# Turning the keys of a decode attention on VectorE instead of TensorE

## The chip, the cores and the metric

The kernel runs on one core of a Trainium2 chip. The metric is the device time of one execution in microseconds, the median of several executions. The profile is of one execution, taken by the hardware profiler; its span runs from the first to the last instruction of the program. The engines are named as the profile names them: PE (TensorE), DVE (VectorE), ACT (ScalarE), POOL (GpSimd), SP (SyncE, whose queue issues nearly all DMAs here).

## The reference

One decode step of grouped-query attention plus a token mixer, both on the same normalised input, in float32:

```python
B, D, HQ, HKV, SK, DH, F = 8, 512, 32, 8, 8192, 128, 1792   # one query position
xn = layernorm(x)                                  # (8, 1, 512)
q  = xn @ wq                                       # 32 query heads of 128
s  = einsum(q, k_cache) * DH**-0.5                 # 4 query heads share a K/V head
o  = softmax(s) @ v_cache                          # over 8192 positions
y  = gelu(layernorm(xn) * w1 + b1) @ w2 + b2       # the mixer: w1 is (1, 1792), w2 (1792, 1)
out = x + o @ wo + y
```

The two caches are (8, 8, 8192, 128) each: 64 pairs of batch element and K/V head, 4 MiB of keys and 4 MiB of values to a pair. Every key and value is used once, for four query rows.

## The kernel before, in words

The 64 pairs are the items, numbered i = h * 8 + b (h the K/V head, b the batch element). A cache tile of an item has 128 partitions and holds 64 rows of 128 numbers in each: partition p has positions 64p to 64p + 63. It comes by one DMA of 4 MiB into one of the five buffers of the pool `ring`. `load_next` (L72) takes the next load of a list that is sorted beforehand (L58 to L61) and is called whenever a buffer has been read for the last time: after an item's last key transpose (L213) and after its last value matmul (L292). SP issues each load as soon as its buffer is free.

The scores need the head dimension on partitions. So keys are transposed first, in chunks of 16 tiles (four chunks an item): `t_half` (L201) does eight 128x128 transposes on PE into a PSUM tile (L209) and copies the 128x1024 result to SBUF (L210), one half of a chunk on ACT, the other on DVE. `qk` (L217) then multiplies: four matmuls a chunk, each with 32 stationary columns and 512 moving ones, into the four 32-row bands of one PSUM tile (L227). The stationary operand is a window on the mostly zero tile Z, which puts the four heads' scores of chunk c into their own rows.

The softmax of an item is a chain of small steps: the row maximum on DVE (L235), a matmul that lays it along the free dimension (L240), a minimum over the rows of the same head on DVE (L243), the exponential with its row sums on ACT (L249), four PE transposes (L256) and a copy on ACT (L257) that make the weights of the value matmuls, and a matmul with a reciprocal (L264, L266) for the sum. `pv` (L272) does four matmuls a chunk (L283). At an item's end ACT scales the result (L296), four small matmuls pick the used blocks (L308), and a DVE copy puts them in the head's tile (L310). After 8 items `o_project` (L312) multiplies with that head's rows of wo (L316) and DVE adds to the sum (L318). The mixer runs beside this, 14 steps a batch element: a GELU on ACT (L335), two operations on POOL (L336, L337).

The order of the work is written out by hand, and each engine executes its instructions in that order. A global step s is one chunk; in each step the order on PE is the two half chunks of transposes of chunk s + 1, `qk` of chunk s, `pv` of chunk s - 9, and what the hooks (L352 to L370) put behind each of these. So three items are in work at a time: one whose keys are turned and multiplied, one in its softmax, one whose values are multiplied. The very last value tile comes in five pieces and its last chunk has matmuls of its own (L288), ahead of the last `o_place`, `o_project` and the output's DMA (L396).

## Time and profile before

| what | value |
|---|---|
| median of 3 runs | 1310.31 us (1308.93 to 1311.67) |
| span of the profiled execution | 1308.7 us |
| that execution against the median of the runs | 1.6 us under it |
| PE, DVE, ACT, POOL busy | 1160.2, 411.6, 586.8, 227.1 us |
| HBM read | 553.69 MB, 423 GB/s over the span |
| mean granted PE clock | 0.962 of full speed |

A matmul in float32 shows as two instructions in the profile, so 16 matmuls are 32 rows; transposes are single. PE's busy time is from modelled ends of pipelined instructions, and the granted clock tells what the throttle let through, 1.00 being full speed. Matmuls that write different 32-row bands overlap: a group of eight instructions (four matmuls) is one unit in the timeline.

### The profile page before, as it was taken

Reading aid. Unit: us, or ns where it says so; the run is one execution under the profiler, and the core shown is the slowest. Engines: PE = TensorE matmul, PEld = TensorE weight load, DVE = VectorE, ACT = ScalarE, POOL = GpSimd, SP = SyncE. Lnnn points to the kernel's source line nnn. Section 1 sums busy time; section 2 is a strip of 40 time slices with the busy share of each in tenths; the row PEclk is TensorE's granted clock in tenths of the full one; section 3 lists DMA queues with packets and bytes.
Section 4 is the critical chain, followed back from the end, with each engine's and each line's share of the span. In section 5 each row is a group of like instructions: output and inputs, shape, how many; then the busy total and the mean of one; then the engine's idle time right before and its main releaser. Section 6 shows DMA issues by size and latency. Waiting matters only on the chain.

```text
span 1308.7 us, 22310 instructions
## 1 busy us (share of the span) xinstructions
PE 1160.2 (89%) x9852; PEld 718.3 (55%) x9852; DVE 411.6 (31%) x640; ACT 586.8 (45%) x734; POOL 227.1 (17%) x242
## 2 busy tenths in 40 slices
PE   3999899988899889988899898899889897999978
PEld 2655555545556555555555555555555555555544
DVE  2433233333233322333323233233233332323321
ACT  0555335553265433554345552455425544345522
POOL 1132102320032200322002220032101221013210
PEclk9999899999999989999899999899989999989999
DMA  9999999999999999999999999999999999999994
GB/s 401 431 431 426 438 432 432 432 431 432 432 432 432 428 430 432 433 431 429 432 430 432 433 431 432 432 432 431 431 433 432 431 431 433 431 434 433 428 428 178
DMA packets 24229, 555.13 MB, mean 424 GB/s; under 512 B 2461, under 2 KB 2493, under 8 KB 6981
## 3 DMA queue, kind: packets, MB, share of 16 engines
q1 hardware_dynamic: 23988, 553.67, 98.5%
q8 instruction: 77, 1.26, 0.4%
q14 instruction: 20, 0.16, 0.0%
q0 software_dynamic: 128, 0.02, 0.0%
q10 hardware_dynamic: 16, 0.02, 0.0%
HBM read 553.69 MB, written 0.02 MB: 423 GB/s over the span
## 4 chain that ended last, share of the span: by engine, by line
DMA 63%; PE 34%; ACT 2%; issue 1%; DVE 0%; SPq 0%; ACTq 0%; DVEq 0%
DMA raw<-in_A_k_cache_dram 62%; PE pt L209 15%; PE acc L227 7%; PE acc L283 6%; PE misc L308 3%; DMA raw<-in_A_wq_dram 2%; ACT L249 1%; PE pt L179 1%; PE misc L325 1%; ACT kt L210 1%; PE misc L316 1%; PE misc L256 0%; ACT t2k L249 0%; PE misc L240 0%; PE misc L264 0%
## 5 line engine op out<-in xcount | busy, mean ns | idle before, releaser
L209 PE MATMUL pt<-ident,raw 128*128 128x128 f32 x4096 | 523.1, 284 | 94.7 <-DMA raw<-in_A_k_cache_dram 93.8
L209 PEld LDWEIGHTS pt<-ident,raw 128*128 128x128 f32 x4096 | 481.8, 148 | 102.8 <-issue 90.8
L210 DVE COPY kt<-pt 128x1024 f32<-128x1024 f32 x256 | 313.5, 1225 | 660.7 <-PE pt L209 531.1
L210 ACT COPY kt<-pt 128x1024 f32<-128x1024 f32 x256 | 258.8, 1011 | 486.0 <-PE pt L209 323.6
L227 PE MATMUL acc<-kt,z 128*32 128x512 f32 x2048 | 283.0, 626 | 0.0
L283 PE MATMUL acc<-raw,pt 128*32 128x512 f32 x2040 | 266.2, 594 | 5.1 <-DMA raw<-in_A_v_cache_dram 5.1
L336 POOL TENSOR_SCALAR g<-g,w2t 128x512 f32<-128x512 f32 x112 | 77.5, 692 | 824.9 <-ACT g L335 824.9
L283 PEld LDWEIGHTS acc<-raw,pt 128*32 128x32 f32 x2040 | 64.9, 111 | 154.4 <-issue 134.1
L337 POOL TENSOR_TENSOR macc<-macc,g 128x512 f32<-128x512 f32 x112 | 142.4, 1271 | 9.3
L335 ACT ACTIVATE g<-hb,b1t,w1t 128x512 f32<-128x512 f32 x112 | 91.1, 813 | 9.8 <-POOL macc L337 9.2
L296 ACT ACTIVATE t2k<-acc,rl 128x512 f32<-128x512 f32 (+1 forms) x65 | 44.1, 679 | 109.0 <-PE acc L283 105.1
L308 PEld LDWEIGHTS misc<-ohu,t2k 128*128 128x128 f32 x512 | 61.9, 191 | 54.2 <-DVE kt L210 35.2
L256 PEld LDWEIGHTS misc<-ident,t2k 128*128 128x128 f32 x256 | 26.8, 140 | 79.4 <-ACT t2k L249 78.5
L308 PE MATMUL misc<-ohu,t2k 128*128 128x4 f32 x512 | 67.5, 255 | 0.6 <-ACT t2k L296 0.6
L227 PEld LDWEIGHTS acc<-kt,z 128*32 128x32 f32 x2048 | 41.1, 110 | 45.9 <-issue 45.9
L256 PE MATMUL misc<-ident,t2k 128*128 128x128 f32 x256 | 42.0, 286 | 22.7 <-ACT t2k L249 22.7
L249 ACT ACT_TABLE_LOAD x48 | 61.6, 1283 | 0.8
L335 ACT ACT_TABLE_LOAD x48 | 61.6, 1283 | 0.8
L257 ACT COPY pt<-misc 128x256 f32<-128x256 f32 x64 | 23.7, 370 | 57.5 <-PE misc L256 57.5
L264 PEld LDWEIGHTS misc<-lr,ohl 128*128 128x128 f32 x128 | 19.0, 188 | 53.7 <-issue 39.4
L240 PEld LDWEIGHTS misc<-ident,mr 128*128 128x128 f32 x128 | 19.0, 187 | 53.7 <-DVE kt L210 38.6
L235 DVE TENSOR_REDUCE mr<-acc 128x1 f32<-128x512 f32 x64 | 43.7, 683 | 7.0 <-PE acc L227 6.8
(68 smaller groups left out, 249.0 us busy)
## 6 DMA issues: line engine op xcount, KB each, us to landing
raw<-in_A_k_cache_dram SPq DMA_DIRECT2D x63, 4096.0 KB, 30.0
raw<-in_A_v_cache_dram SPq DMA_DIRECT2D x63, 4096.0 KB, 33.5
raw<-in_A_wq_dram SPq DMA_DIRECT2D x2, 4096.0 KB, 12.6
wo<-in_A_wo_dram SPq DMA_DIRECT2D x8, 1024.0 KB, 32.4
raw<-in_A_k_cache_dram SPq DMA_DIRECT2D x4, 1024.0 KB, 26.8
raw<-in_A_v_cache_dram SPq DMA_DIRECT2D x1, 2048.0 KB, 30.4
raw<-in_A_v_cache_dram SPq DMA_DIRECT2D x1, 1024.0 KB, 32.5
raw<-in_A_v_cache_dram SPq DMA_DIRECT2D x1, 512.0 KB, 33.2
```

The costliest lines, as they stand in the source:

```text
L209: nc.tensor.transpose(pt[:, t * P:(t + 1) * P], KR[n // NCH][:, n % NCH * CH_T + k * w + t, :], ident)
L210: (nc.vector.tensor_copy if k else nc.scalar.copy)(KT[n][:, k * w * P:(k + 1) * w * P], pt)
L227: nc.tensor.matmul(S[i][j * GW:(j + 1) * GW, :], w, kt[:, j * 512:(j + 1) * 512], start=(c == 0), stop=(c == NCH - 1))
L235: nc.vector.tensor_reduce(mr, S[i], AX.X, ALU.max)
L249: nc.scalar.activation(p, S.pop(i), AF.Exp, bias=st[i], scale=SCALE, accum_out=lr)
L256: nc.tensor.transpose(m[:, u * P:(u + 1) * P], p[:, u * P:(u + 1) * P], ident)
L283: nc.tensor.matmul(O[i][j * GW:(j + 1) * GW, :], w, v[:, j * 512:(j + 1) * 512], start=(c == 0), stop=(c == NCH - 1))
L296: nc.scalar.activation(ob[:, x], o[:, x], AF.Copy, scale=rl)
L308: nc.tensor.matmul(m[:, :REP], ob[:, u * DH:(u + 1) * DH], ohu[:, u * REP:(u + 1) * REP], start=(u == 0), stop=(u == GT - 1))
L335: nc.scalar.activation(g, hb, AF.Gelu_apprx_tanh, bias=b1t[:, j:j + 1], scale=w1t[:, j:j + 1])
L336: nc.gpsimd.tensor_scalar(g, g, w2t[:, j:j + 1], 1.0, op0=ALU.mult, op1=ALU.mult)
L337: nc.gpsimd.tensor_add(acc, acc, g)
```

## The change

The keys are no longer transposed by PE through PSUM. `turn` lets DVE transpose a quarter of an item's keys (128 partitions by 16 tiles of 128, 2048 numbers in each partition) in place in the ring buffer, in blocks of 32x32. After that the head dimension is on partitions only within blocks of 32: partition 32i + d holds component d of a quarter j of the head dimension for the positions of partition band i. So `qk` runs over the four quarters j of the head dimension, with 16 matmuls as before, each reading 16 runs of 32 numbers of the turned tile; its stationary operand W has the query's quarter j in the four bands (`QT` now holds each quarter copied to all bands, by four more matmuls in each half of `q_project`). An item's `qk` starts when its four turns are done, and frees the buffer (`load_next` is called after it).

The softmax keeps its maximum, bias and exponential. Its row sums go to a tile of the head (`LR`). The four transposes and the ACT copy become one matmul with a permutation matrix (512 columns) and one DVE block transpose out of PSUM. The value matmuls are 16 with 512 columns, as before. The result is not scaled on ACT: DVE masks it (128x512), adds halves (256, then 128 columns), one matmul picks, and the scaling by the sums is done once a head (`o_sums`, `o_scale`).

The order is no longer one of chunks with a lag: an item's scores, softmax and values follow one another, and the four turns of the next item stand between them. The last two items have an order of their own. The loads alternate keys and values, except that the last keys come ahead of the last two value tiles; wo of the last head comes behind the last values, in four pieces, and wo of the head before in two.

```diff
@@ load_next, load_wo
-        order.append((i * NCH - 1, kc, KR, i))
-        order.append((i * NCH + LAG, vc, VR, i))
+        order.append((2 * i, kc, KR, i))
+        order.append((2 * i + (1 if i < N_IT - 2 else 2.5), vc, VR, i))
...
+            if not order:
+                load_wo(HKV - 1)
...
+        if h < HKV - 1:
+            for p in (slice(0, 8), slice(8, P)) if h == HKV - 2 else (slice(0, P),):
+                nc.sync.dma_start(t[p], rows[p])
+        else:
+            for r in range(REP):
+                nc.sync.dma_start(t[:, r, :], rows[:, r, :])
@@ t_half goes (PE transposes and the copies to SBUF), turn comes
+    def turn(i, a, w=NT // 4):
+        if i < N_IT:
+            t = KR[i][:, a:a + w, :].rearrange("p t d -> p (t d)")
+            nc.vector.transpose(t, t)
+    def qk(i):
+        h, b = divmod(i, B)
+        S[i] = ps_s.tile([P, 512], F32, name="s")
+        kt = KR.pop(i).rearrange("p (u g) d -> p g u d", g=NG)
+        for j in range(NB):
+            for g in range(NG):
+                nc.tensor.matmul(S[i][g * Q:(g + 1) * Q, :], W[h % 2][:, b, j, :], kt[:, g, :, j * Q:(j + 1) * Q],
+                                 start=(j == 0), stop=(j == NB - 1))
+        load_next()
@@ sm_place: four transposes and an ACT copy go
+        m = misc()
+        nc.tensor.matmul(m, perm, st.pop(i), start=True, stop=True)
+        PT[i] = work.tile([P, 512], F32, name="pt")
+        nc.vector.transpose(PT[i], m)
@@ sm_sum and the scaling on ACT go; four picks become one
+    def o_pick(i):
+        om = t2k.tile([P, 512], F32, name="t2k")
+        nc.vector.tensor_tensor(om.rearrange("p (g d) -> p g d", g=NG), O.pop(i).rearrange("p (g d) -> p g d", g=NG),
+                                dm.unsqueeze(2).to_broadcast([P, NG, DH]), ALU.mult)
+        ob = work.tile([P, 256], F32, name="ob")
+        nc.vector.tensor_add(ob, om[:, :256], om[:, 256:])
+        nc.vector.tensor_add(ob[:, :DH], ob[:, :DH], ob[:, DH:])
+        OB[i] = ob
...
+        nc.tensor.matmul(MH[h][:, b * REP:(b + 1) * REP], OB.pop(i)[:, :DH], sel, start=True, stop=True)
...
+    def o_sums(h):
+        m = misc()
+        for r in range(REP):
+            nc.tensor.matmul(m[:, r * B:(r + 1) * B], sel[:, r:r + 1].to_broadcast([P, P]), LR[h % 2], start=True, stop=True)
+        RD[h] = work.tile([P, REP, B], F32, name="rd")
+        nc.vector.reciprocal(RD[h], m[:, :REP * B].rearrange("p (r b) -> p r b", r=REP))
+
+    def o_scale(h):
+        nc.vector.tensor_tensor(OTS[h % 2].rearrange("p r (b s) -> p r b s", s=BS)[:, :, :, 0],
+                                MH.pop(h)[:, :REP * B].rearrange("p (b r) -> p r b", r=REP), RD.pop(h), ALU.mult)
@@ the order of the work, instead of the hooks and the loop over chunks
+    for i in range(N_IT - 2):
+        h, b = divmod(i, B)
+        if i == 0:
+            for a in range(4):
+                turn(0, a * quart)
+        qk(i)
+        sm_max(i)
+        sm_bias(i)
+        sm_exp(i)
+        sm_place(i)
+        turn(i + 1, 0)
+        pv(i)
+        if b == 0:
+            mx_begin(h)
+        k = 2 if h + 1 < HKV else 3
+        for j in range(k * b, min(k * b + k, NF)):
+            mx_step(h, j)
+        turn(i + 1, quart)
+        o_pick(i)
+        turn(i + 1, 2 * quart)
+        o_place(i)
+        if b == B - 1:
+            o_sums(h)
+            mx_end(h)
+        if b == 2:
+            load_wo(h) if h < HKV - 1 else None
+        if 3 <= b < 3 + NB and h + 1 < HKV:
+            q_place(h + 1, b - 3)
+        turn(i + 1, 3 * quart)
+        if b == B - 1:
+            o_scale(h)
+            o_project(h)
+    h = HKV - 1
+    i, e = N_IT - 2, N_IT - 1
+    qk(i)
+    sm_max(i)
+    sm_bias(i)
+    sm_exp(i)
+    sm_place(i)
+    for a in range(4):
+        turn(e, a * quart)
+    pv(i)
+    qk(e)
+    o_pick(i)
+    sm_max(e)
+    sm_bias(e)
+    sm_exp(e)
+    sm_place(e)
+    o_place(i)
+    o_sums(h)
+    mx_end(h)
+    for u0, u1 in ((0, 8), (8, 12), (12, 14), (14, 16)):
+        pv(e, u0, u1)
+    o_pick(e)
+    o_place(e)
+    o_scale(h)
+    o_project(h)
```

## The prediction

> **What bounds the kernel now.** First the page's head, its slices of DMA rate, and the waits.

> ```profile
> span 1308.7 us, 22310 instructions
> PE 1160.2 (89%) x9852; PEld 718.3 (55%) x9852; DVE 411.6 (31%) x640; ACT 586.8 (45%) x734; POOL 227.1 (17%) x242
> DMA  9999999999999999999999999999999999999994
> GB/s 401 431 431 426 438 432 432 432 431 432 432 432 432 428 430 432 433 431 429 432 430 432 433 431 432 432 432 431 431 433 432 431 431 433 431 434 433 428 428 178
> ...
> q8 instruction: 77, 1.26, 0.4%
> ...
> raw<-in_A_k_cache_dram SPq DMA_DIRECT2D x63, 4096.0 KB, 30.0
> ```
> ```profile
> PE pt L209 <- DMA raw<-in_A_k_cache_dram: 93.8, 43, 5.4
> ```

> The DMA engines are full at 432 GB/s from the second slice to the last but one, and PE, busy as it is, waits 43 times for keys. An item needs 2 x 4.194 MB, which is 19.42 us at 432 GB/s; an eighth of a head's wo (1.05 MB) adds 0.30. So **19.7 us an item** is the floor of any order of the work: a loop that stays under it gains only at the ends, one that goes over it pays 64 times its excess.

> **What the change removes.** 64 PE transposes an item, their copies on two engines, and the overlap of three items. The rows of the groups:

> ```profile
> L209 PE MATMUL pt<-ident,raw 128*128 128x128 f32 x4096 | 523.1, 284 | 94.7 <-DMA raw<-in_A_k_cache_dram 93.8 <-ACT g L335 0.6 <-ACT kt L210 0.2
> ...
> L210 DVE COPY kt<-pt 128x1024 f32<-128x1024 f32 x256 | 313.5, 1225 | 660.7 <-PE pt L209 531.1 <-issue 75.6 <-ACT g L335 46.5
> L227 PE MATMUL acc<-kt,z 128*32 128x512 f32 x2048 | 283.0, 626 | 0.0
> ...
> L235 DVE TENSOR_REDUCE mr<-acc 128x1 f32<-128x512 f32 x64 | 43.7, 683 | 7.0 <-PE acc L227 6.8
> ...
> L318 DVE TENSOR_TENSOR yacc<-misc,yacc 128x128 f32<-128x128 f32 x8 | 2.3, 291 | 5.5 <-PE misc L316 5.5
> ...
> L116 DVE COPY t2k<-oh 128x128 f32<-128x128 f32 x1 | 0.2, 226 | 0.0
> ```

> PE falls by 523 us of transposes. That is worth nothing in itself, since PE is not the floor. What decides is the new order on the in-order engines. On DVE the maximum of item i stands behind the four turns of item i (done in the pass of item i - 1), and waits for `qk`; behind it wait bias, the weights' transpose, two turns, `o_pick`, two turns. On PE `qk` of the next item waits for the last turn. So nothing of two items overlaps except `pv` with two turns, and the period is one closed chain: qk, maximum, bias, minimum, exponential, permutation, transpose, the longer of pv and two turns, pick, two turns.

> **The price of a turn** (2048 columns; no such operation in the trace). DVE needs 683 ns for 512 columns (L235) and 1225 for 1024 (L210), 1.06 ns a column: 1.225 + 1024 x 1.06 ns = 2.31 us. Lower bound: SBUF to SBUF the copy L116 takes 226 ns for 128 columns where L318 takes 291; with the same fixed 155 ns (291 - 128 x 1.06) that is 0.55 ns a column, so 1.3 us. Upper bound: POOL's 1271 ns for 512 columns, quoted below, is 2.48 ns a column, 5.1 us. I take 2.3, the row of the same engine and the longest stream. [...]

> **The other links** come from the last softmax, where nothing but its own chain ran:

> ```profile
> 1287.06 1.07 PE L227 MATMUL acc<-kt,z 128*32 128x512 f32 x8
> ...
> 1287.94 1.04 PE L283 MATMUL acc<-raw,pt 128*32 128x512 f32 x8
> ...
> 1288.19 0.69 DVE L235 TENSOR_REDUCE mr<-acc 128x1 f32<-128x512 f32 x1 [0.86 <-PE acc L227]
> ...
> 1290.89 0.49 PE L240 MATMUL misc<-ident,mr 128*128 128x128 f32 x2
> ...
> 1291.42 0.29 DVE L243 CUSTOM_DVE_ANT_0 sq<-misc,hmask 128x128 f32<-128x128 f32 x1 [1.25 <-PE misc L240]
> ...
> 1291.75 0.69 ACT L249 ACTIVATE t2k<-acc,nb 128x512 f32<-128x512 f32 x1
> ...
> 1292.58 0.66 PE L256 MATMUL misc<-ident,t2k 128*128 128x128 f32 x4 [0.21 <-ACT t2k L249]
> ```
> ```profile
> 47.56 1.12 PE L325 MATMUL misc<-hn,ident 8*128 8x512 f32 x2
> ...
> 48.72 0.59 ACT L327 COPY hb<-misc 128x512 f32<-128x512 f32 x1 [1.86 <-PE misc L325]
> ```

> Groups of four matmuls follow at 0.88 us, and the reader starts 1.13 after the last one: qk or pv is 3 x 0.88 + 1.13 = 3.77. (The moving keys are now 16 runs of 32; L227 and L283 cost alike on contiguous data, the trace bounds this only from below.) Maximum 0.74 with its semaphore; bias 0.53; minimum 0.33; exponential 0.83; permutation, two passes of 512 columns as L325, 1.16; transpose of 512 out of PSUM 0.69; pick 0.69 + 0.42 + 0.29 + 0.05 = 1.45 (512, 256 and 128 columns). At full clock: 3.77 + 0.74 + 0.53 + 0.33 + 0.83 + 1.16 + 0.69 + 4.6 (two turns, over pv's 3.77) + 1.45 + 4.6 = **18.7 us**. Beside it, per head:

> ```profile
> L196 DVE COPY z<-qt x16: 174/179/1287, 34.3 to 1071.9; 128x32 f32<-128x32 f32 x16
> ```
> ```profile
> L337 POOL TENSOR_TENSOR macc<-macc,g 128x512 f32<-128x512 f32 x112 | 142.4, 1271 | 9.3
> ```
> ```profile
> 1304.08 1.08 PE L316 MATMUL misc<-wo,ot 128*32 128x128 f32 x32 [0.26 <-DVE ot L310]
> 1305.23 0.29 DVE L318 TENSOR_TENSOR yacc<-misc,yacc 128x128 f32<-128x128 f32 x1 [1.20 <-PE misc L316]
> 1305.55 0.69 SPq L396 DMA_DIRECT2D out_dram<-yacc  x1
> ```

> Eight placing copies at about 0.25 (four times L196's columns, a quarter of its partitions; its longest, 1287 ns, is as long as a POOL addition) and, at the last item, projection 1.15 plus four short DVE operations of 0.29 at most: (2.0 + 2.3) / 8 = 0.55 an item. Sum 19.25, under 19.7. So at full clock the DMA would stay the floor, by half a microsecond.

> **The clock** is what speaks against it. Nine windows at the throttle's own boundaries (PE busy first, granted clock after POOL):

> ```profile
> 189.91:193.32 3.41, 1.04 (x10) 0.73 (x7) 0.17 (x1) 0.00 (x0) 0.00 (x0) 1.00 0.94 404
> 193.32:196.74 3.42, 3.42 (x19) 2.67 (x20) 0.46 (x1) 1.01 (x1) 0.00 (x0) 0.50 1.00 431
> 196.74:200.15 3.41, 3.41 (x25) 1.17 (x17) 1.46 (x2) 0.58 (x1) 0.00 (x0) 1.00 1.00 432
> 1104.68:1108.10 3.42, 0.44 (x6) 0.30 (x2) 0.17 (x1) 0.00 (x0) 0.00 (x0) 1.00 1.02 441
> 1108.10:1111.51 3.41, 2.29 (x11) 2.32 (x12) 0.00 (x0) 0.27 (x1) 0.00 (x0) 0.50 1.07 461
> 1111.51:1114.92 3.41, 3.41 (x19) 1.55 (x21) 1.35 (x2) 0.74 (x1) 0.00 (x0) 0.50 1.04 447
> 1114.92:1118.34 3.42, 3.42 (x32) 2.62 (x24) 0.74 (x2) 0.60 (x1) 0.00 (x0) 1.00 0.99 422
> 1241.22:1244.63 3.41, 1.72 (x18) 0.50 (x10) 1.04 (x2) 1.90 (x2) 1.31 (x2) 1.00 0.91 390
> 1244.63:1248.05 3.42, 1.85 (x16) 1.73 (x16) 0.00 (x0) 0.71 (x1) 0.64 (x1) 1.00 1.04 434
> ```
> ```profile
> 1112.80 1.94 PE L227 MATMUL acc<-kt,z 128*32 128x512 f32 x8
> ...
> 1114.50 1.24 PE L283 MATMUL acc<-raw,pt 128*32 128x512 f32 x8
> ```

> A window with PE busy 1.04 of 3.41 us is followed by one at half clock; one with 1.72 is not. Back at full clock it goes after a window filled to 3.41, not after one with 2.29. At half clock a group takes 1.70 (1112.80 to 1114.50) instead of 0.88. The new loop has about 3.5 + 3.5 + 1.2 us of PE work in 19.7, 42%, and it lies badly: from the end of pv to the next qk are pick and two turns, 6.05 us with one four-column matmul. Wherever the boundaries fall, one window there has at least half of these, 3 us, idle. So every qk starts at half clock. Between qk and pv are 4.3 us with bias and permutation in them, some 1.3 busy: mostly the same. A burst starting at a random place runs slow to the end of its own window if it fills most of that (one start in five, 3.1 us), or through the next one too (4.8 us on average): 4.4 together, of which half, 2.15 us, is lost. qk and pv become 5.9, bias and permutation 0.1 and 0.4 longer.

> [...]

> **The sum.** 5.9 + 0.74 + 0.63 + 0.33 + 0.83 + 1.56 + 0.69 + 5.9 (over two turns' 4.6) + 1.45 + 4.6 = 22.6, and 0.55: **23.2 us an item**, 3.5 over the floor. Start: the first keys are there at about 34 and DVE comes to them at 38, behind the larger query projection; four turns: 47. Then 62 x 23.2 = 1438. The last two items, from the first's qk: 5.9 + 4.8 to the permuted weights, four turns 9.2 beside pv, qk 5.9, 4.8, pv 5.9, then pick, place, scale, project and add 3.5, and the output 3.2 as above (1305.55 to the span's end): 43. Span 1528; the profiled execution of before lies 1.6 under its median, so **1530 us**.

> **Costed at nothing**, with cover: the loads (SP's issue for the next key buffer now waits for qk's end, with the load for the next value buffer behind it; but with a loop slower than the DMA the ring is full; if the loop were faster, three tiles are under way, 29 us of transfer, against a wait of about 15 from keys landed to qk's end); wo's order and pieces (six more issues on SP, behind which only the output waits); the mixer, two steps an item: GELUs, POOL and table switches need some 6 us of the 18 between two exponentials; without that cover up to 1.3 an item. The trimmed tail matters only if the DMA is the floor.

> **Rivals.** (a) The clock costs under 0.5 us an item and DMA stays the floor. For it: 19.25 against 19.7, and DVE has no other work. Against: all the windows above. The end: the last values landed at 1263.8 + 33.5 = 1297.3 (rows below); wo now behind them frees 2.4, half of the instructions' 1.26 MB (q8) at 432 GB/s 1.5; then last matmuls 0.7, pick 1.45, place 0.5, scale 0.3, projection and addition 1.45, output 3.2: span 1301, **1303 us**, faster. It decides where the chain is under 19.7 us.

> ```profile
> L81 SPq DMA_DIRECT2D raw<-in_A_v_cache_dram x68: 327/328/1469, 31.6 to 1263.8; - x68
> ```
> ```profile
> raw<-in_A_v_cache_dram SPq DMA_DIRECT2D x2, 256.0 KB, 33.5
> ```

> (b) The clock falls only once an item, before qk: pv hides under two turns, the permutation is at full clock, 22.6 - 1.3 - 0.5 = 20.8, 21.4 with the rest: 47 + 62 x 21.4 + 41 = **1415 us**. (c) Turns at the lower bound 1.3: 22.6 - 2.0 + 0.55 = 21.1, **1390 us**. (d) Turns at the upper bound 5.1: both pairs 10.2, 32.5 + 0.55: about **2170 us**.

> **Chances.** Forecast 0.48 (its own range 1470 to 1585), (a) 0.27, (b) 0.12, (c) 0.08, (d) 0.03, no change to be measured 0.02. A measurement of this kernel tells 0.2%, 2.6 us, from no change. Faster 0.26, same 0.03, slower 0.71. The range takes in (a) to (c): 1298 to 1580, leaving out a fast end, a loop that locks on seven windows of 3.41 us (23.9, about 1573) with a slow start, and (d).

> **What would show it.** Granted clock about 0.7 and below 0.8 with first groups of each qk at 1.70; DMA share near 0.85 in all slices; DVE waiting for PE at the maximum and at the pick; turns at 2.3. A granted clock above 0.95, or turns well under 2 us, would make it wrong; so would a DMA share of 9 in all slices.

## The result, and the profile after

The changed kernel takes **1578.6 us** (median of 4 runs, 1576.5 to 1579.0); the kernel before, on the same chip, 1311.0 (median of 4). The ratio is **1.2045**, 95% interval 1.2028 to 1.2062: slower by 268 us, where the prediction said 219. First the page's head and its slices.

```profile
span 1576.9 us, 12454 instructions
...
PE 928.2 (59%) x5172; PEld 267.0 (17%) x5172; DVE 796.9 (51%) x835; ACT 289.0 (18%) x364; POOL 229.5 (15%) x244
...
PEclk9676677776777767776677776776768777776768
DMA  9999888998888988899889988899888998898880
GB/s 407 430 432 389 353 333 348 370 387 333 346 357 365 370 346 359 345 376 371 334 333 377 382 346 346 342 363 386 360 333 345 374 369 350 333 369 336 336 330 1
...
raw<-in_A_k_cache_dram SPq DMA_DIRECT2D x63, 4096.0 KB, 12.3
```

The loads are no longer the limit: most slices show 333 to 390 GB/s where before had 431, and a load of keys lands 12.3 us after its issue instead of 30.0: SP now issues a load only every 12 us or so (a load of values at 727.02 us, one of keys at 739.45), so little is queued ahead of it. But no engine is full either: PE 59%, DVE 51%. The row PEclk (the granted clock of TensorE in tenths) is mostly sixes and sevens: 0.736 in the mean, where the kernel before had 0.962. Time that nothing fills is waiting, and the chain says whose. One item of it, from the chain of waits of the changed kernel between 724 and 752 us (start, length, what):

```profile
727.02 0.70 DVE mr L232
...
727.77 0.50 PE misc L237 x2
...
728.40 0.29 DVE sq L240
...
728.78 1.28 ACT L246
...
730.08 0.79 ACT t2k L246 x2
...
730.91 1.34 PE misc L253 x2
...
732.27 0.73 DVE pt L255
...
733.05 6.39 PE o L266 x32
...
739.46 0.70 DVE t2k L277
...
740.99 0.39 PE mh L288 x2
741.37 4.67 issue
746.04 5.01 PE s L222 x32
...
751.07 0.70 DVE mr L232
```

From maximum to maximum it is 24.05 us, and every link of the predicted chain is there, in its order. The 4.67 us called "issue" are PE waiting for nothing that this view can name. The timeline of the same place names it:

```profile
740.85 2.30 DVE L212 STREAM_TRANSPOSE raw<-raw 128x2048 f32<-128x2048 f32 x1
...
743.17 0.45 DVE L205 COPY w<-qt 32x128 f32<-32x128 f32 x2
743.63 2.31 DVE L212 STREAM_TRANSPOSE raw<-raw 128x2048 f32<-128x2048 f32 x1
```

Two turns, with two copies of the next head's queries between them; the score product (746.04 in the chain) follows. The groups give the means, and beside them stands the one link that the prediction did not have:

```profile
L212 DVE STREAM_TRANSPOSE raw<-raw 128x2048 f32<-128x2048 f32 x256 | 577.1, 2282 | 0.3
L222 PE MATMUL s<-raw,w 128*32 128x512 f32 x2048 | 359.3, 864 | 254.0 <-issue 221.8
L266 PE MATMUL o<-raw,pt 128*32 128x512 f32 x2048 | 370.3, 890 | 51.0 <-DVE pt L255 51.0
...
L246 ACT ACT_TABLE_LOAD x55 | 70.6, 1283 | 799.7 <-DVE nb L240 799.6
L253 PE MATMUL misc<-t2k,perm 128*128 128x512 f32 x128 | 96.2, 840 | 147.5 <-ACT t2k L246 147.5
```
```profile
L249 ACT ACT_TABLE_LOAD x48 | 61.6, 1283 | 0.8
```

In the trace a load of a table (ACT_TABLE_LOAD) stands before each exponential that follows a GELU, and before each GELU that follows an exponential (54 of each in the changed kernel). The exponential's table is loaded in 55 of 64 items, the first one, ahead of which no GELU ran, among them. In the kernel before ACT stood idle for 0.8 us in all ahead of these loads; now for 799.7, of which 799.6 end with the minimum (nb). The 799.7 us cost nothing by themselves. What costs is the 1.28 us that begin when they end: in the chain above, 728.78 to 730.08. The list of waits says how many loads are caught so:

```profile
ACT L246 <- DVE nb L240: 799.6, 47, 21.2
...
ACT t2k L246 <- DVE nb L240: 243.1, 17, 22.6
```

47 loads begin only when the minimum is there. In the other 17 items it is the exponential itself that waits: nine need no load, and in eight, the second item of each head, the load runs right behind the GELU (460.31 us), 7.5 us ahead of its exponential (467.85), and costs nothing. What sets these eight apart was not tried.

### The profile page after: what moved, and what is told of

It is laid out like the page before. It is cut to its first block, busy times and chain, and to the rows that moved or that the text cites. A ratio compares the mean times of both kernels' runs of the same rounds, so it can differ in the third digit from the quotient of the medians.

```text
span 1576.9 us, 12454 instructions
## 1 busy us (share of the span) xinstructions
PE 928.2 (59%) x5172; PEld 267.0 (17%) x5172; DVE 796.9 (51%) x835; ACT 289.0 (18%) x364; POOL 229.5 (15%) x244
## 4 chain that ended last, share of the span: by engine, by line
PE 59%; issue 17%; DVE 15%; ACT 7%; DMA 1%; DVEq 0%; ACTq 0%; SPq 0%
PE o L266 24%; PE s L222 23%; PE misc L253 6%; ACT L246 4%; ACT t2k L246 3%; DVE pt L255 3%; DVE mr L232 3%; DVE t2k L277 3%; DVE raw L212 2%; PE misc L237 2%; DVE ob L280 2%; DMA raw<-in_A_wq_dram 1%; PE mh L288 1%; DVE ob L281 1%; DVE sq L240 1%
## 5 line engine op out<-in xcount | busy, mean ns | idle before, releaser
L212 DVE STREAM_TRANSPOSE raw<-raw 128x2048 f32<-128x2048 f32 x256 | 577.1, 2282 | 0.3
L222 PE MATMUL s<-raw,w 128*32 128x512 f32 x2048 | 359.3, 864 | 254.0 <-issue 221.8
L266 PE MATMUL o<-raw,pt 128*32 128x512 f32 x2048 | 370.3, 890 | 51.0 <-DVE pt L255 51.0
L328 POOL TENSOR_SCALAR g<-g,w2t 128x512 f32<-128x512 f32 x112 | 77.7, 694 | 1071.9 <-ACT g L327 1071.9
L232 DVE TENSOR_REDUCE mr<-s 128x1 f32<-128x512 f32 x64 | 44.3, 691 | 363.4 <-PE s L222 363.4
L246 ACT ACT_TABLE_LOAD x55 | 70.6, 1283 | 799.7 <-DVE nb L240 799.6
L253 PE MATMUL misc<-t2k,perm 128*128 128x512 f32 x128 | 96.2, 840 | 147.5 <-ACT t2k L246 147.5
L222 PEld LDWEIGHTS s<-raw,w 128*32 128x32 f32 x2048 | 90.0, 152 | 466.7 <-issue 433.7
L255 DVE STREAM_TRANSPOSE pt<-misc 128x512 f32<-128x512 f32 x64 | 45.9, 717 | 217.4 <-PE misc L253 217.4
L266 PEld LDWEIGHTS o<-raw,pt 128*32 128x32 f32 x2048 | 82.1, 155 | 351.8 <-issue 227.3
L327 ACT ACTIVATE g<-hb,b1t,w1t 128x512 f32<-128x512 f32 x112 | 91.1, 813 | 127.4 <-POOL macc L329 126.7
L277 DVE TENSOR_TENSOR t2k<-o,dm 128x512 f32<-128x512 f32 x64 | 44.2, 691 | 100.8 <-PE o L266 100.8
L246 ACT ACTIVATE t2k<-s,nb 128x512 f32<-128x512 f32 x64 | 44.0, 687 | 243.6 <-DVE nb L240 243.1
L327 ACT ACT_TABLE_LOAD x54 | 69.3, 1283 | 1.4
L240 DVE CUSTOM_DVE_ANT_0 sq<-misc,hmask 128x128 f32<-128x128 f32 x64 | 18.6, 291 | 44.2 <-PE misc L237 44.2
## 6 DMA issues: line engine op xcount, KB each, us to landing
raw<-in_A_v_cache_dram SPq DMA_DIRECT2D x63, 4096.0 KB, 12.8
raw<-in_A_k_cache_dram SPq DMA_DIRECT2D x63, 4096.0 KB, 12.3
raw<-in_A_wq_dram SPq DMA_DIRECT2D x2, 4096.0 KB, 17.1
```

What stands on the lines that cost most here:

```text
L212: nc.vector.transpose(t, t)
L222: nc.tensor.matmul(S[i][g * Q:(g + 1) * Q, :], W[h % 2][:, b, j, :], kt[:, g, :, j * Q:(j + 1) * Q], start=(j == 0), stop=(j == NB - 1))
L232: nc.vector.tensor_reduce(mr, S[i], AX.X, ALU.max)
L246: nc.scalar.activation(p, S.pop(i), AF.Exp, bias=st[i], scale=SCALE, accum_out=LR[h % 2][:, b:b + 1])
L253: nc.tensor.matmul(m, perm, st.pop(i), start=True, stop=True)
L255: nc.vector.transpose(PT[i], m)
```

## The experiments

Two theories had to be told apart from the start. **Theory**: one item's steps wait for each other in a closed line, TensorE's links in it run partly at half clock, and the table load is one more link. **Rivals**: the turned keys are slow to read (16 runs of 32), the turns are too much work, or the clock itself is the bound. Times below are medians, "before" is the kernel before in the same session (1310.3 to 1311.5 us), intervals are 95%.

### 1. TensorE kept busy

```diff
+    def extra(n):      # n groups of 4 matmuls, 128x32 by 512, into a tile that nobody reads
...
         sm_exp(i)
+        extra(2)
         sm_place(i)
         turn(i + 1, 0)
         pv(i)
+        extra(1)
...
         o_place(i)
...
+        extra(4)
```

> The changed kernel with TensorE kept busy while it waits: groups of four 128x32 x 512 matmuls whose result no instruction reads, two groups an item behind the exponential's issue, one behind the value product, four behind the placing of the result. Nothing of the changed kernel is left out. Theory (an open chain whose TensorE links run at a halved clock because TensorE idles for more than half of the item): the granted clock goes above 0.95 (0.736 without the groups), the score product and the value product take 3.8 and 4.6 us instead of 5.7 and 5.9, the permutation 1.2 instead of 1.55; the item falls from 24.0 to about 20.3 us and the time to 50 + 62 x 20.3 + 36 = 1345 us (1320 to 1400). Rival (the longer products come from the keys' strided columns or from the turns sharing the keys' memory, and the clock has no part in it): the products keep their 5.7 and 5.9 us, and the time stays at 1577 us or grows by the added matmuls.

Measured: **1365.9 us**, 1.0419 (1.0403 to 1.0434). More work on TensorE makes the kernel 213 us faster. The two products in the groups of this run:

```profile
L231 PE MATMUL s<-raw,w 128*32 128x512 f32 x2048 | 240.5, 610 | 57.6 <-issue 54.0
L275 PE MATMUL o<-raw,pt 128*32 128x512 f32 x2048 | 236.4, 602 | 51.0 <-DVE pt L264 51.0
```

The score product's mean falls from 864 ns to 610, the value product's from 890 to 602, although the keys lie just as they did. So the clock made them long, not the strided columns or the turns beside them. The granted clock is 0.982. The time is 21 us above the forecast, 0.3 an item. In the trace it lies at the heads' ends: from an item's maximum to the next are 18.8 to 20.5 us within a head (a little less at the very end), but 24.2 to 26.8 behind its last item. What takes the time there was not tried.

### 2. The table loaded early

```diff
         for j in range(k * b, min(k * b + k, NF)):
             mx_step(h, j)
+        nc.scalar.activation(pre[:, 1:2], pre[:, 0:1], AF.Exp)   # one column, read by nobody
```

> The changed kernel with one added ScalarE instruction an item: an exponential of a single column, whose result no instruction reads, behind the mixer's gelu steps, so that the table of the exponential is loaded while ScalarE waits for nothing. Nothing is left out. Theory (the table load that stands between the minimum and the exponential is a link of the chain, 1.36 us there against 0.33 without it): the item falls by 1.03 us to 22.96, and the time to about 1513 us (1490 to 1525). Rival (the items stay locked to the clock's windows, 56 of them in eight items, so that what one link gives up is lost in waiting or in slower matmuls): 1577 us, the period of eight items stays 191.1 us.

Measured: **1543.0 us**, 1.1769 (1.1751 to 1.1786). Neither: 36 us of the 64 came. The table load is off the chain (its line idles 1.0 us in all), and TensorE's groups took part of the gain back:

```profile
L224 PE MATMUL s<-raw,w 128*32 128x512 f32 x2048 | 386.8, 925 | 255.7 <-issue 223.5
L268 PE MATMUL o<-raw,pt 128*32 128x512 f32 x2048 | 344.3, 834 | 50.9 <-DVE pt L257 50.9
...
L255 PE MATMUL misc<-t2k,perm 128*128 128x512 f32 x128 | 114.1, 988 | 88.3 <-ACT t2k L248 88.3
...
L378 ACT ACT_TABLE_LOAD x54 | 69.3, 1283 | 1.0
```

Score product 864 to 925 ns, permutation 840 to 988, value product 890 to 834. TensorE's instructions are the same in both; the change lies in where they start within the clock's windows: for the score products of one head, between 0.02 and 0.60 of a window in the changed kernel and between 0.20 and 0.93 in this run, and the same in each of the six heads between the first and the last. The timeline shows how firmly the loop is tied to the windows: the maximum of an item and of the one eight later, in the changed kernel and in this run.

```profile
703.07 0.69 DVE L232 TENSOR_REDUCE mr<-s 128x1 f32<-128x512 f32 x1 [5.35 <-PE s L222]
```
```profile
894.22 0.69 DVE L232 TENSOR_REDUCE mr<-s 128x1 f32<-128x512 f32 x1 [5.35 <-PE s L222]
```
```profile
708.98 0.69 DVE L234 TENSOR_REDUCE mr<-s 128x1 f32<-128x512 f32 x1 [6.62 <-PE s L224]
```
```profile
896.71 0.69 DVE L234 TENSOR_REDUCE mr<-s 128x1 f32<-128x512 f32 x1 [6.62 <-PE s L224]
```

191.15 us and 187.73 us. A window of the throttle is 3.413 us in the prediction's rows (six of them are 20.48 us in those at the end of this document), and in the trace of the changed kernel 255 of the 256 stretches of one granted clock, all but the final one, are a whole number of windows long; so these are 56.0 and 55.0 windows. The loop falls into step with the windows, eight items at a time (single items run from 22.1 to 25.7 us), and the link taken out of it paid one whole window: 3.4 us for eight items, where six loads of 1.28 us, 7.7, were taken out. For the 48 items from the seventh to the 55th maximum that makes 20.5 us; the rest of the 36 came in the first and last items, where the step does not hold.

### 3. Both

```diff
+        extra(1)   # behind the exponential; 1 behind pv, 4 behind o_place
...
+        nc.scalar.activation(pre[:, 1:2], pre[:, 0:1], AF.Exp)
```

> Both additions at once: the added matmul groups (one behind the exponential's issue, one behind the value product, four behind the placing of the result; nobody reads them) and the early exponential of one column. Nothing is left out. Theory (chain and table load add up): the chain is 20.3 - 1.0 = 19.3 us an item, below the 19.7 us in which the loads can bring one item; the time falls back on the loads, 1303 to 1320 us, level with the kernel before, with the DMA share at 9 tenths in every slice. Rival (turning keys by VectorE costs time by itself, beside clock and table): 1380 us or more.

Measured: **1327.6 us**, 1.0123 (1.0106 to 1.0140). The slices of the rate in this run:

```profile
GB/s 398 437 428 423 432 432 430 430 427 431 428 432 433 426 428 429 434 431 426 429 429 434 428 429 431 428 432 427 431 431 428 430 360 396 433 431 428 430 427 118
```

The loads are the floor again, at the rate of before in nearly every slice, so the theory's sum holds. The 7.6 us over its upper end (1320) can be put down to slices 33 and 34: 360 and 396 GB/s for 33.1 us each cost (72 + 36) / 432 x 33.1 = 8.3 us. Runs 7 to 10 show where that comes from.

### 4. The same instructions with two items in work

```diff
-        order.append((2 * i + (1 if i < N_IT - 2 else 2.5), vc, VR, i))
+        order.append((2 * i + (2.5 if i != N_IT - 3 else 4.3), vc, VR, i))
...
     for i in range(N_IT - 1):
         h, b = divmod(i, B)
+        turn(i + 1, 0)
         qk(i)
+        turn(i + 1, quart)
         sm_max(i)
         sm_bias(i)
         sm_exp(i)
-        sm_place(i)
-        turn(i + 1, 0)
-        pv(i)
+        turn(i + 1, 2 * quart)
+        pv(i - 1)                 # from the second item on
...                                # mixer steps, one item later
+        turn(i + 1, 3 * quart)
+        o_pick(i - 1)
+        sm_place(i)
+        o_place(i - 1)            # at a head's end o_sums, mx_end, o_scale, o_project
...                                # an end of its own for the last item
```

> The changed kernel with another order and the same instructions: two items are in work, the turns of item i+1 run while the softmax of item i is computed, the value product of item i-1 stands behind the bias matmul of item i, its picking behind the turns; a load of keys is issued before the values that are needed an item later. Nothing is added to keep the clock up and the table load stays where it was. Theory (what costs the time is that one item's steps wait for each other in one line, not the work): per item TensorE needs some 15 us at a halved clock and VectorE 12.5 us (four turns 9.1), both below the 19.7 us of the loads, so the time falls to 1303 to 1320 us although the granted clock stays low (below 0.85). Rival (the halved clock or the turns are themselves the bound): 1400 us or more.

Measured: **1320.0 us**, 1.0072 (1.0055 to 1.0089). Page and waits of this run:

```profile
DMA  9999999999999999999999999999999999999994
```
```profile
DVE raw L212 <- DMA raw<-in_A_k_cache_dram: 317.2, 61, 10.3
```

259 us come back with the same turns and matmuls, at a granted clock of 0.798. The DMA engines are full in every slice but the last, and DVE now waits 61 times for keys, which no engine did in the changed kernel. So neither the turns nor the halved clock is the bound; their place in one line was.

### 5. Only the pick taken out of the line

```diff
     for i in range(N_IT - 2):
         qk(i)
+        end_of(i - 1)             # o_place, and at a head's end sums, scale, projection
...
-        o_pick(i)
         turn(i + 1, 2 * quart)
-        o_place(i)
...
         turn(i + 1, 3 * quart)
+        o_pick(i)
```

> The changed kernel with the picking of a result moved behind all four turns, and the placing of it, with the sums and the projection of a group of eight, behind the next score product; same instructions. Theory (one closed line of waits sets the item): the value product and the picking leave the line, which is then score product 5.7 + maximum 0.75 + bias 0.63 + table and exponential 2.2 + permutation 1.55 + transpose 0.8 + four turns 9.2 and the picking 1.5 behind them, 21.2 to 22.4 us an item, so 1404 us (1390 to 1480). Rival (the two-item order gains because VectorE's turns run while the loads land, not because the line gets shorter): 1577 us.

Measured: **1366.6 us** (two runs, 1357.2 and 1376.0), 1.0429 (1.0362 to 1.0497). Chain of waits of this run:

```profile
782.50 5.37 PE s L222 x32
...
798.87 4.25 issue
803.12 5.37 PE s L222 x32
```

20.62 us from score product to score product, against 24.05. The direction is the theory's; the time is below the forecast's lower end of 1390, because I let the pick (1.5 us) stand in the line. In this run it lies under the next score product (802.94 to 804.38 us). The 4.25 us of "issue" before the next score product are what is left of the four turns behind the value product.

### 6. The turns left out

```diff
-            nc.vector.transpose(t, t)
+            if a == 0:
+                nc.vector.transpose(t[:, :32], t[:, :32])
```

> The changed kernel with nearly all of the turning left out: one 32-column block of each load of keys is turned in place of all 256, so the scores are taken from keys that are not turned. The order and all other instructions stay. Theory (two of the four turns, 4.6 us, stand on the line of waits between the picking and the next score product): the item falls from 24.0 by 4.6 us or more, to 19.4, which is below what the loads need; 1310 to 1335 us. Rival (the turns lie beside the value product and the loads, and what is slow is TensorE's halved clock and the waits between engines): 1480 us or more.

Measured: **1322.9 us**, 1.0096 (1.0077 to 1.0114), with the DMA share at 9 in every slice but the last and a granted clock of 0.778. Without the two turns the line is shorter than the loads need, half clock or not.

### 7 to 11. The loads, and the end

A part of the change that the prediction costed at nothing turned up here. In run 7 the kernel before gets only the new order and pieces of wo:

```diff
@@ the kernel before, load_next and load_wo
+            if not order:
+                load_wo(HKV - 1)
...
+            for p in (slice(0, 8), slice(8, P)) if h == HKV - 2 else (slice(0, P),):
+                nc.sync.dma_start(t[p], rows[p])
```

> The kernel before with one part of the change alone: the last output weights loaded behind the last values, in four pieces, and those ahead of them in two. Nothing is left out. Theory (the end of the kernel before runs from the landing of the last keys through TensorE's work): the last keys land 2.4 us earlier (1.05 MB at 432 GB/s) and the time falls by that, 1308.2 us. Rival (the end hangs on the last bytes of all, whose number stays the same): no change, 1310.5 us.

Measured: **1315.1 us**, 1.0039 (1.0027 to 1.0052), slower, which neither theory had. In run 8 the two-item order got a better end:

```diff
     sm_exp(e)
-    for j in range(2 * (B - 2), NF):
-        mx_step(h, j)             # done two items earlier now
-    sm_place(e)
     pv(e - 1)
+    sm_place(e)
     o_pick(e - 1)
```

> The order with two items in work, and its end put right: the last mixer steps done two items earlier, and the value product of the last item but one right behind the last score product instead of behind the softmax, so that the last value product can follow its last piece of values. Same instructions, nothing left out. Theory (the two-item order is bound by the loads, and 14 us lay between their last landing and the end against 11.4 us in the kernel before): about 6 us less than the 1320 us of that order, 1314 us; below the kernel before (1304 us) if the slow stretch of the loads near 1075 us (two items of 25 us in place of 19.4) does not come again. Rival (the end is set by TensorE's own work at a halved clock): 1320 us.

Measured: **1315.2 us**, 1.0037 (1.0025 to 1.0049): 4.8 us less, where about 6 were expected from the end, and the slow stretch came again (slice 33 of the rate at 327 GB/s). It lies at the same place in two kernels, this one and that of run 7, that share little but the load of wo for the last head but one, in 8 and 120 rows. So that was undone in both, as the only edit, in runs 9 (two-item order) and 10 (kernel before):

```diff
-            for p in (slice(0, 8), slice(8, P)) if h == HKV - 2 else (slice(0, P),):
-                nc.sync.dma_start(t[p], rows[p])
+            nc.sync.dma_start(t, rows)
```

> The two-item order with the mended end, and the output weights of the last group but one loaded in one piece of 128 rows instead of two of 8 and 120. Nothing else differs. Theory (the slow stretch of the loads near 1075 us, where the sixteen DMA engines are all busy and move 250 to 300 GB/s instead of 431, belongs to the piece of 120 rows that starts there): the stretch goes, some 8 us of loads with it, and the time falls from 1315 to about 1307 us. Rival (the slow stretch belongs to the place of the data or to something outside the kernel): it stays, 1315 us.

> The kernel before with the last output weights loaded behind the last values, as in the run that was 0.4% slower, and those ahead of them in one piece as in the kernel before. Nothing is left out. Theory (the two pieces cost some 8 us of loads, and the later load of the last weights brings the last keys 2.4 us earlier): 1307 to 1308 us, 2 to 3 us below the kernel before. Rival (loading the last weights last is what costs): 1315 us.

Measured: the two-item order **1310.6 us**, 0.9994 (0.9982 to 1.0006), ten runs between 1305.8 and 1312.1; the kernel before with wo last **1306.1 us**, 0.9967 (0.9954 to 0.9979). Both fall as the theory has it, by 4.6 and 9.0 us. The two-item order stays 3.6 us above its forecast of 1307, though its slow stretch is gone (slice 33 at 423 GB/s); run 11 finds 5.9 us in its end. Windows of the kernel before with wo last, in two pieces and in one (us, then the engines' busy time, granted clock, DMA share, GB/s):

```profile
1070.00:1080.00 10.00, 10.00 (x86) 5.79 (x82) 4.30 (x9) 4.32 (x5) 3.23 (x4) 0.95 1.02 300
1080.00:1090.00 10.00, 5.19 (x46) 2.88 (x38) 1.48 (x3) 4.55 (x7) 2.17 (x3) 0.90 1.00 310
1090.00:1100.00 10.00, 7.66 (x42) 4.97 (x43) 1.92 (x3) 1.72 (x2) 1.96 (x2) 0.59 1.02 305
```
```profile
1070.00:1080.00 10.00, 9.49 (x83) 6.01 (x80) 4.45 (x8) 5.39 (x7) 3.38 (x4) 1.00 0.99 418
1080.00:1090.00 10.00, 8.19 (x71) 4.93 (x70) 3.22 (x4) 5.20 (x6) 3.08 (x4) 1.00 1.01 429
1090.00:1100.00 10.00, 7.71 (x68) 4.92 (x71) 2.92 (x5) 4.77 (x6) 0.82 (x1) 1.00 1.03 441
```

The DMA engines count as full in both, but in two pieces they move 300 to 310 GB/s for 30 us: 30 x 125 / 430 = 8.7 us lost, against 9.0 us between the medians. No run here shows why the engines move less; the two pieces were not tried apart. Loading the last wo last does what the first theory had expected of it, and more: 4.2 us under the kernel before, 2.4 expected.

Run 11 is the two-item order with whole loads and a shorter end:

```diff
-        order.append((2 * i + (2.5 if i != N_IT - 3 else 4.3), vc, VR, i))
+        order.append((2 * i + ({N_IT - 4: 4.1, N_IT - 3: 4.3}.get(i, 2.5)), vc, VR, i))
...
+    mx_end(h)
     qk(e)
...
     sm_place(e)
+    o_sums(h)
     o_pick(e - 1)
-    o_place(e - 1)
-    o_sums(h)
-    mx_end(h)
     for u0, u1 in ((0, 8), (8, 12), (12, 14), (14, 16)):
         pv(e, u0, u1)
+    o_place(e - 1)
```

> The two-item order with whole weights, the keys of item 62 loaded ahead of the values of item 60, and the end written shorter: the mixer's sum ahead of the last score product, the sums of the exponentials between the last permutation and its transpose, the last value product ahead of the placing of item 62. Same instructions. Theory (after the loads run undisturbed, the end is 26.8 us of waits from the last score product on, of which some 5 us are other items' work standing in line, and the loads' own end leaves room for it): 1302 to 1304 us, 0.5% below the kernel before. Rival (the end is bound by the landing of the last values, which nothing here moves): level with the run before it, 1307 us.

Measured: **1304.7 us**, 0.9957 (0.9944 to 0.9969). This is the change made to pay: 0.43% under the kernel before and 17% under the change as it came, with the same matmuls and turns. Of the 0.43%, 0.33% can be had in the kernel before by loading the last wo last; the turns on DVE, the two-item order and its shorter end bring 1.4 us beside that. The five runs of each do not overlap (1304.3 to 1305.5, 1305.9 to 1306.8), so the gain is probably there, but it is 0.1%, and which of the three brings it was not tried.

### 12. The changed kernel with whole loads

The edit is that of runs 9 and 10, made to the changed kernel.

> The changed kernel with the output weights of the last group but one in one piece of 128 rows instead of two of 8 and 120; nothing else differs. Theory (the line of waits sets the item, and a load that is 8 us late is hidden because loads take only 86% of the time): no change, 1578 us (1574 to 1582), although the same edit took 9.0 us from a kernel that is bound by its loads. Rival (the late loads stop the line near 1075 us): 1570 us.

Measured: **1576.5 us**, 1.2031 (1.2010 to 1.2053); the changed kernel had 1.2045 (1.2028 to 1.2062). No change that can be told: what cost 9.0 and 4.6 us where loads bind is hidden where they do not.

## Why the prediction was right, and where it was not

The direction and the mechanism held, the closed chain and TensorE's half clock in it; one link was missing from the chain, and 1578.6 lies just under the upper end of 1580 that the prediction gave. By its steps:

- **The floor of 19.7 us an item** and "a loop that goes over it pays 64 times its excess": right. Runs 3, 4 and 6 fall back on it.
- **The closed chain**: right, link for link, as the chain of waits shows; runs 4 and 5 take links out and the time follows.
- **The price of a turn**, 2.31 us from the maximum's and the copy's rate: 2.282 measured. Both bounds (1.3 and 5.1), and with them rivals (c) and (d), are out.
- **The clock**: granted 0.736, forecast about 0.7. qk and pv at 5.9 us, from a burst that starts at a random place in the windows: 5.03 and 6.41 us with their semaphores in the item shown (746.04 to 751.07, 733.05 to 739.46), together 11.4 where 11.8 were forecast, and run 1 shows the whole excess to be the clock's. The windows of that item (PE busy first, granted clock after POOL):

```profile
725.01:728.43 3.42, 2.44 (x22) 0.70 (x14) 0.72 (x2) 0.00 (x0) 0.00 (x0) 1.00 0.85 287
728.43:731.84 3.41, 0.93 (x2) 0.30 (x2) 0.27 (x2) 3.03 (x4) 0.00 (x0) 0.98 0.78 336
731.84:735.25 3.41, 2.60 (x13) 0.59 (x16) 2.98 (x3) 1.21 (x3) 1.97 (x2) 0.50 1.02 442
735.25:738.67 3.42, 3.42 (x20) 0.79 (x16) 2.13 (x1) 0.73 (x1) 1.96 (x2) 0.52 0.76 326
738.67:742.08 3.41, 1.10 (x10) 0.30 (x2) 2.55 (x4) 0.00 (x0) 0.00 (x0) 0.98 0.54 154
742.08:745.49 3.41, 0.00 (x0) 0.00 (x0) 3.38 (x4) 0.00 (x0) 0.00 (x0) 0.50 1.07 461
```

```profile
L222 PE MATMUL s<-raw,w x32: 593/1061/1062, 50.1 to 56.0; 128*32 128x512 f32 x32
```
```profile
1537.27 5.30 PE L222 MATMUL s<-raw,w 128*32 128x512 f32 x32 [4.07 <-issue]
```

  (1537.27 - 50.1) / 62 = 23.99. 62 x 0.79 = 49 us, and that is the miss. Start 50 (47 forecast) and end 39.6 (43) cancel. The table load, 47 x 1.28 / 64 = 0.94 an item, is more than the 0.79; the other links came out 0.15 shorter together. That is a sum of links, by which 60 us would come back without the loads. 36 came (run 2), since TensorE's groups and the step with the windows took part of it; 1543.0 is still 13 above the forecast.
- **Loads costed at nothing**: right in this kernel (run 12). The prediction's "wo now behind them frees 2.4" in rival (a) did not see that the two pieces of the wo ahead cost 9 where the loads are the floor.

## What to carry to other kernels

Work moved to an idle engine pays only if its place in the order lets another item's work run beside it: write down, for each in-order engine, what stands in front of the instruction that the next engine waits for, and close the loop. Read a link's price off a place where everything that will run between two of its instances also ran; the last item of a kernel is the place where least does. When a chain is long and TensorE idles in it, reorder first: a second item in work was worth 259 us, keeping the clock up with empty matmuls 213, loading a table early 36.

## What the runs showed of the hardware that was not expected

- ACT's table load often waits for the same minimum as the exponential that needs it, though it can do without: 47 of 55 loads of 1283 ns begin when the minimum is there, eight begin right behind the GELU, one of these 7.5 us ahead of its exponential (460.31, 467.85). One column of exponential ahead of it takes the load off the line (run 2).
- A loop that is slowed by TensorE's clock can lock to the throttle's windows: 56.0 windows for eight items, 55.0 with 7.7 us of table loads taken out of them. The saving was then one step of 3.41 us; no other step was seen.
- Splitting one load of 1 MB by rows into 8 and 120 cost 9.0 us of a kernel bound by its loads (1315.1 against 1306.1) and 4.6 of another (1315.2 against 1310.6), in the first at a DMA share of 1.00 to 1.02 in the slow stretch. The share tells that engines are occupied, not that they move what they can.
